# Block attention before a low-rank mixer: the masked fourth of the scores left out from step twelve on, with v and part of the mask turned

## The chip, the cores and the metric

The kernel runs on one core of one Trainium2 chip. The metric is the device time of one execution in microseconds (us). Four executions of the kernel before took 671.55, 673.17, 673.52 and 674.01 us; their median is 673.34 us.

The engines are named as in the profile: PE is TensorE (PEld its weight loads), DVE is VectorE, ACT is ScalarE, POOL is GpSimd and SP the queue that issues the DMA transfers. SBUF is the on-chip memory, PSUM the memory that PE writes its products to. Each has 128 partitions (rows).

## What is computed

Inputs are q, k and v of 4 batches, 8 heads, 768 positions and 64 features, a decay `lam` per head, and the weights of a mixer. The first half is linear attention with decay, written here in the reference's blocks:

```python
intra = einsum('bhic,bhjc->bhij', qb, kb) * Dmask      # Dmask[i,j] = lam**(i-j) for i >= j, else 0
intra = einsum('bhij,bhjd->bhid', intra, vb)
inter = einsum('bhid,bhde->bhie', qb * lam_pow, kv_state)
out[block] = intra + inter
kv_state = lam_block * kv_state + einsum('bhsd,bhse->bhde', kb * rev_pow, vb)
```

The output, as x of 4 x 768 x 512, goes through `u = x + (x^T U V)^T` (rank 32) and then `u + relu(u @ w_ch1) @ w_ch2` with an inner width of 2048.

What matters here is `Dmask`: a score whose key j comes after its query i is multiplied by zero.

## The kernel before

The kernel takes 128 positions at a time. With 4 batches of 6 such tiles there are 24 steps, numbered s = 0 to 23; c = s mod 6 is the place of the step in its batch. Two heads lie side by side in the 128 partitions of the transposed q and k: head 2a + x has pair number a = 0..3 and half x = 0, 1. The attention stage of all 24 steps ends at about 121 us; after it come two large matrix products of the mixer (lines 717 to 899), in which the kernel spends the rest of its time. The change doesn't touch those.

One step issues the following, in an order that `pieces` (lines 554 to 581) writes out by hand. Every engine works through its own instructions strictly in that order.

- `prep(s+1)`, lines 349 to 367: PE transposes q and k of the next tile into PSUM (pq, pk), ACT copies them to SBUF (qt, kt). The loads of later tiles are issued on SP.
- `scale`: POOL multiplies q and k by powers of the decay (qs, ks).
- `fade` (line 392): ACT multiplies the state by the decay of one tile, in four small instructions (faded).
- `mix` (line 514): PE forms the rank-32 part of a tile seven steps back (pu), DVE adds it to that tile (x_nat, line 517).
- `low`, `low_rows`: only where c = 0, the projection of the batch before (pp, L469), split by DVE and ACT into parts.
- `intra(s)` (line 453): PE multiplies the masked scores sm with v into px; ACT copies px to SBUF (x_nat, line 458).
- `state(s)` (line 418): for c < 5, PE forms k^T v (pkv), DVE adds it to the faded state (kv). The PSUM bank of pkv is that of pk, so pkv starts only after ACT has copied kt. Then the next tile of v is loaded into the buffer that has come free.
- `scores(s+1)` (line 400): PE multiplies k with q into pss, keys in the partitions and queries in the columns.
- `aside`: pieces of work for the weights of the large products (lines 149 to 224) on DVE; their ACT part follows as `late`.
- `inter(s+1)` (line 441): PE multiplies qs with the state kv into px.
- `masked(s+1)` (line 409): DVE multiplies pss with the mask, one instruction for each half x, and writes sm.
- `turn` (lines 531 to 547): PE transposes the finished tile (put), DVE splits it (ut, u_hl), ACT and POOL finish the split one step later (u_hl at line 550, u_d).

All these matmuls are in fp32, and each leaves two records of weight load and two of matmul in the trace (the transposes one). A matmul whose weights are 64 x 64 uses one quarter of the array; which one follows from the partitions of its operands and of its output. From step 12 on the scores of a tile are already formed by 16 such matmuls, two halves of keys for each head, each with all 128 queries; before step 12 by 8 matmuls with 128 keys each:

```python
for rows in half if s >= 2 * NT else [slice(0, P)]:
    nc.tensor.matmul(
        out=pss[rows, x, a, :], lhsT=kt[half[x], a, rows],
        rhs=qt[half[x], a, :], start=True, stop=True,
```

For keys 64 to 127 the first 64 of these 128 columns are scores that the mask sets to zero: a fourth of the tile's scores.

Of the kernel before, what the change touches and what calls it, by code (L numbers as in the profile page):

```python
# [8 lines left out]
FP32 = mybir.dt.float32  # L9
# [5 lines left out]
P = 128  # L15
# [3 lines left out]
def kernel(  # L19
# [28 lines left out]
    nc = tc.nc  # L48

    B, H, S, D = q.shape  # L50
    HP = H // 2
    NT = S // P
# [45 lines left out]
    def tmp(name):  # L98
        return wconv.tile([P, C], FP32, tag="tmp", bufs=3, name=name)
# [146 lines left out]
    att = att_ctx.enter_context(tc.tile_pool(name="att", bufs=1))  # L246
# [5 lines left out]
    def two_banks(name, tag):  # L252
        return psf.tile([P, 2, N], FP32, tag=tag, name=name)
# [12 lines left out]
    raw = {}  # L266
# [30 lines left out]
    mask = consts.tile([P, 2, HP, P], FP32, name="mask")  # L297
# [33 lines left out]

    xs = {}
    st = {}
    kv = {}
    half = [slice(0, D), slice(D, P)]
# [55 lines left out]

    def scores(s):
        qt, kt = st[s]["qt"], st[s]["kt"]
        st[s]["pss"] = pss = two_banks("pss", "pss").rearrange("p x (a i) -> p x a i", a=HP)
        for a in range(HP):
            for x in range(2):
                for rows in half if s >= 2 * NT else [slice(0, P)]:
                    nc.tensor.matmul(  # L400
                        out=pss[rows, x, a, :], lhsT=kt[half[x], a, rows],
                        rhs=qt[half[x], a, :], start=True, stop=True,
                    )

    def masked(s):
        pss = st[s].pop("pss")
        st[s]["sm"] = sm = att.tile([P, 2, HP, P], FP32, tag="sm", bufs=1, name="sm")
        for x in range(2):
            nc.vector.tensor_tensor(out=sm[:, x], in0=pss[:, x], in1=mask[:, x], op=ALU.mult)  # L409

    def state(s):
# [34 lines left out]
    def intra(s):  # L446
        first = s % NT == 0
        sm, vr, px = st[s]["sm"], raw[s, "v"], st[s]["px"]
        px = px[:, :, 0 : HP * D].rearrange("p x (a e) -> p x a e", a=HP)
        for a in range(HP):  # L450
            for x in range(2):
                for t in range(2):
                    nc.tensor.matmul(  # L453
                        out=px[half[t], x, a, :], lhsT=sm[:, x, a, half[t]],
                        rhs=vr[:, 2 * a + x, :], start=(first and a == 0), stop=(a == HP - 1),
                    )
        xs[s] = x_pool.tile([P, C], FP32, tag="x", name="x_nat")
        nc.scalar.copy(xs[s].rearrange("p (a x e) -> p x a e", a=HP, x=2), px)


    pps = {}
# [57 lines left out]
    uhl, ud, turned = {}, {}, {}  # L519
# [42 lines left out]
    for s in range(NS):  # L562
        b, c = divmod(s, NT)
        done = s - NT - 1
        more = s + 1 < NS
        step = [("prep", s + 1), ("scale", s + 1)] * more + [("fade", s)] * (c == 1)
        step += [("late", s - 1)] * (s == NT)
        step += [("mix", done)] * (0 <= done < NS - NT - 1)
        step += [("low", b - 1)] * (c == 0 and b > 0)
        step += [("low_rows", b - 1)] * (c == 0 and b > 0)  # L570
        step += [("intra", s)]
        step += [("next_of_low", b - 1)] * (c == 0 and b > 0)
        step += [("late", s)] * (s < NT - 1 or s == NT) + [("state", s)]
        step += [("next_of_low", b - 1)] * (c == 0 and b > 0)
        step += [("turned", done - 1)] * (done > 0) + [("late", s)] * (done >= 0)
        step += [("next_of_low", b - 1)] * (c == 0 and b > 0)
        step += [("scores", s + 1)] * more
        step += [("aside", s)] * (s >= 2 * NT)
        step += [("inter", s + 1), ("masked", s + 1)] * more
        step += [("fade", s + 1)] * (more and c > 0)  # L580
        step += [("aside", s)] * (s < 2 * NT)
        step += [("turn", done)] * (done >= 0 and done // TG < FG)
        pieces += step
    waiting = {name: list(range(NS)) for name in "qkv"}

    def load_next(name, engine=nc.sync):
# [3 lines left out]

    run = {
        "prep": prep, "fade": fade, "scores": scores, "masked": masked, "inter": inter,
        "intra": intra, "state": state,
        "low": low, "low_rows": low_rows, "next_of_low": next_of_low, "mix": mix, "turn": turn,
        "scale": scale, "turned": lambda s: turned.pop(s)(),
    }
    def v_steps():

# [186 lines left out]
    c0, b = NS - NT, B - 1  # L785
# [181 lines left out]
```

## Time and profile before

| what | value |
|---|---|
| median of four executions | 673.34 us |
| the profiled execution | 673.52 us, of which the span from first to last instruction is 671.7 us |
| granted PE clock | 1.000 |
| busy share of the span | PE 99%, DVE 74%, ACT 41%, POOL 17% |
| one step of the attention stage (71.84 to 76.58 us) | 4.74 us, of which DVE is busy 4.71 and ACT 4.09 |
| scores, steps 12 to 23 | 192 matmuls of 64x128 (384 records), one record 0.269 us |
| masking, steps 12 to 23 | 24 DVE instructions of 128x512, 0.680 us each |
| ACT copy of 128x512 from PSUM | 0.585 to 0.592 us |

How to read it: the length of a matmul record is its passage through the pipeline, and records overlap, so what a block of matmuls costs is the time from its first start to the first start of the next block. A busy engine need not be the bound: PE also counts as busy while matmuls trickle. The number in brackets behind an instruction is idle time of its engine before it, with the instruction that ended it.

### The profile page before, as it was taken

Reading aid. Unit: us, or ns where it says so; the run is one execution under the profiler, and the core shown is the slowest. Engines: PE = TensorE matmul, PEld = TensorE weight load, DVE = VectorE, ACT = ScalarE, POOL = GpSimd, SP = SyncE. Lnnn points to the kernel's source line nnn. Section 1 sums busy time; section 2 is a strip of 40 time slices with the busy share of each in tenths; the row PEclk is TensorE's granted clock in tenths of the full one; section 3 lists DMA queues with packets and bytes.
Section 4 is the critical chain, followed back from the end, with each engine's and each line's share of the span. In section 5 each row is a group of like instructions: output and inputs, shape, how many; then the busy total and the mean of one; then the engine's idle time right before and its main releaser. Section 6 shows DMA issues by size and latency. Waiting matters only on the chain.

```text
span 671.7 us, 13171 instructions
## 1 busy us (share of the span) xinstructions
PE 664.8 (99%) x5124; PEld 544.9 (81%) x5124; DVE 497.2 (74%) x873; ACT 277.7 (41%) x517; POOL 112.6 (17%) x92
## 2 busy tenths in 40 slices
PE   9999999999999999999999999999999999999997
PEld 8887989788888888888888888888888888888885
DVE  5688999877999777777797265786586775865854
ACT  4675767554555444444454121332222322322320
POOL 4555657340000000000000000030030300300300
PEclk9999999999999999999999999999999999999999
DMA  9999994254676555555587899854363363542421
GB/s 204 216 221 223 243 242 118 89 210 156 238 279 235 204 203 204 204 203 204 203 282 256 313 318 390 284 197 138 94 211 102 111 203 94 162 152 95 160 91 62
DMA packets 131775, 131.27 MB, mean 195 GB/s; under 512 B 81346, under 2 KB 89794, under 8 KB 131714
## 3 DMA queue, kind: packets, MB, share of 16 engines
q1 hardware_dynamic: 130656, 130.18, 61.2%
q8 instruction: 40, 0.66, 0.4%
q10 hardware_dynamic: 1058, 0.26, 0.2%
q14 instruction: 21, 0.17, 0.1%
HBM read 80.09 MB, written 50.33 MB: 194 GB/s over the span
## 4 chain that ended last, share of the span: by engine, by line
PE 96%; DVE 2%; ACT 1%; issue 0%; DVEq 0%; ACTq 0%
PE pz L731 27%; PE pz L866 13%; PE pz L864 13%; PE pd L741 13%; PE pd L868 13%; PE pss L400 3%; PE px L453 3%; PE put L531 2%; PE pq L355 1%; PE pkv L418 1%; PE px L441 1%; PE pk L355 1%; PE pp L469 1%; DVE sm L409 1%; PE pu L514 1%; PE idle L343 0%
## 5 line engine op out<-in xcount | busy, mean ns | idle before, releaser
L731 PE MATMUL pz<-u_hl,w 128*128 128x512 f32 x768 | 190.4, 398 | 0.0
L731 PEld LDWEIGHTS pz<-u_hl,w 128*128 128x128 f32 x768 | 144.1, 188 | 35.4 <-issue 0.4
L866 PE MATMUL pz<-w_hl,m 128*128 128x512 f32 x384 | 151.1, 396 | 0.0
L864 PE MATMUL pz<-w_hl,m 128*128 128x512 f32 x384 | 151.0, 397 | 0.0
L868 PE MATMUL pd<-w_d,m 128*128 128x512 f32 x384 | 149.5, 397 | 0.0
L847 ACT ACTIVATE m<-mt 128x512 fp32r<-128x512 f32 x96 | 60.6, 632 | 197.0 <-PE pd L868 137.7
L848 DVE SCALAR_TENSOR_TENSOR m<-rm,m 128x512 fp32r<-128x512 f32 x96 | 71.4, 745 | 50.0 <-ACT m L847 49.7
L893 POOL TENSOR_TENSOR o<-o,u 128x512 f32<-128x512 f32 x20 | 29.8, 1526 | 447.4 <-DVE o L889 447.4
L746 DVE SCALAR_TENSOR_TENSOR r<-pd,r 128x512 f32<-128x512 f32 x96 | 61.8, 685 | 53.3 <-ACT r L737 38.8
L741 PE MATMUL pd<-u_d,w 128*128 128x512 f32 x384 | 98.6, 397 | 0.0
L737 ACT ACTIVATE r<-pz 128x512 f32<-128x512 f32 x96 | 52.1, 595 | 93.0 <-PE pz L731 92.9
L866 PEld LDWEIGHTS pz<-w_hl,m 128*128 128x128 f32 x384 | 72.4, 188 | 17.6
L864 PEld LDWEIGHTS pz<-w_hl,m 128*128 128x128 f32 x384 | 72.3, 188 | 17.6
L868 PEld LDWEIGHTS pd<-w_d,m 128*128 128x128 f32 x384 | 72.3, 188 | 17.6
L741 PEld LDWEIGHTS pd<-u_d,w 128*128 128x128 f32 x384 | 72.1, 188 | 17.3
L849 DVE SCALAR_TENSOR_TENSOR m<-m 128x512 fp32r<-128x512 f32 x96 | 69.0, 720 | 0.9
L846 DVE TENSOR_SCALAR mt<-rm 128x512 uint32<-128x512 uint32 x96 | 46.1, 481 | 31.0 <-DMA rm<-r_d 30.4
L409 DVE TENSOR_TENSOR sm<-pss,mask 128x512 f32<-128x512 f32 x48 | 30.8, 684 | 7.0 <-PE pss L400 6.8
L212 ACT CAST w<-wt 128x512 fp32r<-128x512 f32 x32 | 19.8, 620 | 30.5 <-DVE wt L209 23.4
L453 PEld LDWEIGHTS px<-vraw,sm 128*64 128x64 f32 x768 | 24.6, 138 | 5.9 <-DVE sm L409 2.3
L383 POOL TENSOR_TENSOR qs<-qt,powq 128x512 f32<-128x512 f32 x20 | 25.9, 1296 | 20.2 <-ACT qt L358 18.6
L453 PE MATMUL px<-vraw,sm 128*64 128x64 f32 x768 | 28.2, 226 | 0.4 <-DVE sm L409 0.3
(88 smaller groups left out, 681.8 us busy)
## 6 DMA issues: line engine op xcount, KB each, us to landing
r_d<-r SPq DMA_DIRECT2D x96, 256.0 KB, 2.7
rm<-r_d SPq DMA_DIRECT2D x96, 256.0 KB, 2.7
words<-in_moe_w_ch_dram SPq DMA_DIRECT2D x30, 512.0 KB, 4.5
w_d<-w SPq DMA_DIRECT2D x16, 768.0 KB, 3.3
w_hl<-w_d SPq DMA_DIRECT2D x16, 512.0 KB, 6.2
vraw<-in_v_dram SPq DMA_DIRECT2D x24, 256.0 KB, 5.1
u_d<-x_nat SPq DMA_DIRECT2D x24, 256.0 KB, 3.7
u<-u_d SPq DMA_DIRECT2D x24, 256.0 KB, 4.2
```

What stands on the lines that cost most here:

```text
L453: nc.tensor.matmul(out=px[half[t], x, a, :], lhsT=sm[:, x, a, half[t]], rhs=vr[:, 2 * a + x, :], start=(first and a == 0), stop=(a == HP - 1),
L731: nc.tensor.matmul(out=acc[g][0], lhsT=w[:, n, ct, :], rhs=uhl[g][:, n, ct, :], start=(ct == 0 and n == 0), stop=(ct == CT - 1 and n == 1),)
L737: nc.scalar.mul(rs[g], acc[g][0], 4096.0 + 1.0)
L741: nc.tensor.matmul(out=acc[g][1], lhsT=w[:, 2, ct, :], rhs=ud[g][:, ct, :], start=(ct == 0), stop=(ct == CT - 1),)
L746: nc.vector.scalar_tensor_tensor(rs[g], acc[g][1], 4096.0, rs[g], ALU.mult, ALU.add)
L846: nc.vector.tensor_scalar(t.bitcast(U32), r.bitcast(U32), HI, None, ALU.bitwise_and)
L847: nc.scalar.activation(out=m[:, 0], in_=t, func=AF.Relu)
L848: nc.vector.scalar_tensor_tensor(m[:, 1], r, 0.0, hi, ALU.max, ALU.subtract)
L849: nc.vector.scalar_tensor_tensor(m[:, 2], hi, E, low, ALU.mult, ALU.subtract)
L864: nc.tensor.matmul(out=pz, lhsT=m[:, 0, cols], rhs=hl[:, 0], start=first, stop=False)
L866: nc.tensor.matmul(out=pz, lhsT=m[:, 1, cols], rhs=hl[:, 1], start=False, stop=end)
L868: nc.tensor.matmul(out=pd, lhsT=m[:, 2, cols], rhs=dd, start=first, stop=end)
```

## The change

From step 12 on (`TURNED`):

- `scores` leaves out the block of keys 64 to 127 by queries 0 to 63. The keys 0 to 63 still get 128 columns, the keys 64 to 127 get 64.
- For odd pairs of heads (a = 1, 3) the two halves of keys trade places in PSUM: keys 64 to 127 lie in partitions 0 to 63 and the others in 64 to 127. In the loop over output halves o, even pairs have the long matmul first and odd pairs the short one. Each quarter of the array gets two long and two short matmuls.
- The part of pss that is not written keeps what an earlier step left there; the mask multiplies it by zero. For that pss becomes one tile for all steps, `sums`.
- The mask's odd pairs are turned the same way, once: ACT copies their halves crosswise into a spare tile in steps 9 and 10, and back in step 11 (`turn_mask`).
- v of the odd pairs must be turned too, in every step from 12 on: `turn_v`, two ACT copies of 64 partitions by 256 elements. They are issued behind `intra` of the step before; for the second step of a batch (c = 1: steps 13 and 19) they are issued in the step itself, behind the copies of q and k and ahead of `fade`.
- `intra` takes the pairs in the order 0, 2, 1, 3 (in all steps) and reads the turned v for odd pairs.
- `masked` is one DVE instruction of 128x1024 instead of two of 128x512.

In the order of the built program this adds 27 ACT instructions (24 of turn_v, 3 of turn_mask) and takes 12 away on DVE; the counts of matmuls stay. The second half of `intra` now also waits for ACT, and SP's load of v into a used buffer waits for ACT besides PE.

```diff
+    sums = two_banks("pss", "pss")
+    TURNED = 2 * NT
...
-        st[s]["pss"] = pss = two_banks("pss", "pss").rearrange("p x (a i) -> p x a i", a=HP)
+        st[s]["pss"] = pss = sums.rearrange("p x (a i) -> p x a i", a=HP)
         for a in range(HP):
             for x in range(2):
-                for rows in half if s >= 2 * NT else [slice(0, P)]:
+                for o in range(2) if s >= TURNED else ():
+                    i = o if a % 2 == 0 else 1 - o
+                    cols = slice(i * D, P)
                     nc.tensor.matmul(
-                        out=pss[rows, x, a, :], lhsT=kt[half[x], a, rows],
+                        out=pss[half[o], x, a, cols], lhsT=kt[half[x], a, half[i]],
+                        rhs=qt[half[x], a, cols], start=True, stop=True,
+                    )
+                if s < TURNED:
+                    nc.tensor.matmul(
+                        out=pss[:, x, a, :], lhsT=kt[half[x], a, :],
                         rhs=qt[half[x], a, :], start=True, stop=True,
                     )
...
-        for x in range(2):
+        for x in [slice(0, 2)] if s >= TURNED else [slice(0, 1), slice(1, 2)]:
             nc.vector.tensor_tensor(out=sm[:, x], in0=pss[:, x], in1=mask[:, x], op=ALU.mult)
...
-        for a in range(HP):
+        for a in (0, 2, 1, 3):
...
-                        rhs=vr[:, 2 * a + x, :], start=(first and a == 0), stop=(a == HP - 1),
+                        rhs=vs[s][:, a // 2, x, :] if s >= TURNED and a % 2 else vr[:, 2 * a + x, :],
...
+    def turn_v(s):
+        odd = raw[s, "v"].rearrange("p (j b x) d -> p j b x d", b=2, x=2)[:, :, 1]
+        vs[s] = att.tile([P, HP // 2, 2, D], FP32, tag="vs", name="vs")
+        for i in range(2):
+            nc.scalar.copy(vs[s][half[1 - i]], odd[half[i]])
+
+    odd_mask = mask[:, :, 1::2, :]
+
+    def turn_mask(n):
+        if n == 0:
+            held.append(tmp("turned").rearrange("p (x j i) -> p x j i", x=2, j=HP // 2))
+        if n < 2:
+            nc.scalar.copy(held[0][half[1 - n]], odd_mask[half[n]])
+        else:
+            nc.scalar.copy(odd_mask, held.pop())
...
+        step += [("turn_v", s)] * (c == 1 and s >= TURNED) + [("fade", s)] * (c == 1)
...
+        step += [("turn_mask", 2)] * (s == TURNED - 1)
+        step += [("intra", s)] + [("turn_v", s + 1)] * (more and s + 1 >= TURNED and c > 0)
+        step += [("turn_mask", s - TURNED + 3)] * (TURNED - 3 <= s < TURNED - 1)
```

More of the change, by code (lines that the diff above doesn't have):

```diff
@@ L326 @@
     r_pool = None
+    sums = two_banks("pss", "pss")
+    TURNED = 2 * NT
     xs = {}
+    vs, held = {}, []
     st = {}
@@ L454, in intra @@
                         out=px[half[t], x, a, :], lhsT=sm[:, x, a, half[t]],
-                        rhs=vr[:, 2 * a + x, :], start=(first and a == 0), stop=(a == HP - 1),
+                        rhs=vs[s][:, a // 2, x, :] if s >= TURNED and a % 2 else vr[:, 2 * a + x, :],
+                        start=(first and a == 0), stop=(a == HP - 1),
                     )
@@ L458, in intra @@
         nc.scalar.copy(xs[s].rearrange("p (a x e) -> p x a e", a=HP, x=2), px)
+        vs.pop(s, None)
+    def turn_v(s):
[11 more added lines that the diff above has]
+            nc.scalar.copy(odd_mask, held.pop())
     pps = {}
@@ L565 @@
         more = s + 1 < NS
-        step = [("prep", s + 1), ("scale", s + 1)] * more + [("fade", s)] * (c == 1)
+        step = [("prep", s + 1), ("scale", s + 1)] * more
+        step += [("turn_v", s)] * (c == 1 and s >= TURNED) + [("fade", s)] * (c == 1)
         step += [("late", s - 1)] * (s == NT)
@@ L570 @@
         step += [("low_rows", b - 1)] * (c == 0 and b > 0)
-        step += [("intra", s)]
+        step += [("turn_mask", 2)] * (s == TURNED - 1)
+        step += [("intra", s)] + [("turn_v", s + 1)] * (more and s + 1 >= TURNED and c > 0)
+        step += [("turn_mask", s - TURNED + 3)] * (TURNED - 3 <= s < TURNED - 1)
         step += [("next_of_low", b - 1)] * (c == 0 and b > 0)
@@ L594 @@
         "low": low, "low_rows": low_rows, "next_of_low": next_of_low, "mix": mix, "turn": turn,
-        "scale": scale, "turned": lambda s: turned.pop(s)(),
+        "turn_v": turn_v, "turn_mask": turn_mask, "scale": scale, "turned": lambda s: turned.pop(s)(),
     }
```

## The prediction

> **What bounds the kernel now.** I read four views in this order: the page's engine totals, the busy time by stretches (one stretch per step of the attention stage), the timelines of TensorE (PE) and ScalarE (ACT) around steps 9 and 13, and the chain of waits.
>
> The totals and two stretches first. The columns of a stretch are its length, then busy time of PE, its weight loads, VectorE (DVE), ACT and POOL.
>
> ```profile
> PE 664.8 (99%) x5124; PEld 544.9 (81%) x5124; DVE 497.2 (74%) x873; ACT 277.7 (41%) x517; POOL 112.6 (17%) x92
> ...
> 71.84:76.58 4.74, 4.74 (x126) 4.36 (x126) 4.71 (x8) 4.09 (x14) 3.93 (x4) 1.00 1.08 263
> 81.31:86.15 4.84, 4.82 (x127) 4.37 (x126) 4.80 (x8) 3.25 (x10) 2.78 (x2) 1.00 1.01 247
> ```
>
> Only the attention stage, to about 121 us, is touched. There PE sets the pace of most steps, one every 4.74 us, but DVE is nearly as full (4.71 and 4.80), and ACT fills 4.09 of the first. A saving on PE therefore helps only where neither of the two is late next.
>
> PE, with start, length, line and tile:
>
> ```profile
> 71.84 1.15 PE L453 MATMUL px<-vraw,sm 128*64 128x64 f32 x32
> 72.83 0.64 PE L418 MATMUL pkv<-vraw,ks 128*64 128x64 f32 x16
> 73.39 1.10 PE L400 MATMUL pss<-qt,kt 64*64 64x128 f32 x32
> 74.32 0.64 PE L441 MATMUL px<-kv,qs 64*64 64x64 f32 x32
> 74.89 0.66 PE L531 MATMUL put<-ident,x_nat 128*128 128x128 f32 x4
> ```
>
> Scores occupy 0.93 us (73.39 to 74.32). The product with the state (L441) has the same 32 records on the same four 64x64 quarters of the array (corners, below), with 64 columns instead of 128, and takes 0.57.
>
> ACT at step 9 has no idle time between 52.78 and the end of kt, and PE waits for that kt:
>
> ```profile
> 52.78 0.58 ACT L458 COPY x_nat<-px 128x512 f32<-128x512 f32 x1 [2.19 <-PE pss L400]
> 53.27 0.63 ACT L550 ACTIVATE u_hl<-ut 128x512 fp32r<-128x512 f32 x1
> ...
> 55.17 1.05 ACT L392 ACTIVATE faded<-kv,powq 128x64 f32<-128x64 f32 x4
> 56.13 0.56 ACT L358 COPY qt<-pq 128x512 f32<-128x512 f32 x1
> 56.60 0.57 ACT L358 COPY kt<-pk 128x512 f32<-128x512 f32 x1
> ...
> 57.22 0.69 PE L418 MATMUL pkv<-vraw,ks 128*64 128x64 f32 x16 [0.28 <-ACT kt L358]
> ```
>
> ACT at step 13, with two prices of small copies:
>
> ```profile
> 71.34 0.59 ACT L358 COPY qt<-pq 128x512 f32<-128x512 f32 x1
> 71.82 0.59 ACT L358 COPY kt<-pk 128x512 f32<-128x512 f32 x1
> ...
> L621 ACT CAST vp<-vt 32x384 fp32r<-32x384 f32 x2 | 1.0, 510 | 0.0
> L358 ACT COPY qt<-pq 128x256 f32<-128x256 f32 x2 | 0.7, 372 | 1.7 <-PE pq L355 1.6
> ```
>
> The chain of waits from 78 to 87 us runs through DVE, not PE:
>
> ```profile
> 78.74 1.21 DVE w L217
> 79.95 1.20 DVE sm L409 x2
> ...
> 84.07 1.42 DVE sc L160
> 85.49 1.21 DVE sm L409 x2
> 86.74 1.03 PE px L453 x28
> ```
>
> **Scores.** Blocks 12 to 23 keep 16 matmuls each, but half of them have 64 columns; each corner gets two long and two short ones. The 32 records come in eight rounds of four. Starts take 1.10 - 0.27 (one record) = 0.83 over seven gaps at 128 columns, 0.64 - 0.22 = 0.42 over seven at 64: 0.119 and 0.060, the first inflated by the fill of the first round. I take 0.05 per shortened round, four of them: 0.20 us a block, if each corner runs through its own list. The other bound is that records start in program order over the corners. With 0.11 a long and 0.06 a short record, the first corner of a pair of heads starts at 0, 0.11, 0.22 (short), 0.28 (short), and its neighbour's short ones stand behind its long ones: 0.01, 0.12, then long at 0.23 and 0.34; the second pair likewise from 0.35, but with its short ones at 0.45 and 0.51 behind the neighbour's last long one, to 0.80 in all. Now it is 8 x 0.11 = 0.88, with own lists 0.68. So 0.08 saved. Bounds: 0 and 0.23.
>
> That all 32 records fit 0.93 us speaks for own lists: 16 matmuls leave 32 records, so two for each corner in turn; if the second of a corner held up the next corner's first, sixteen times 0.11 would already be 1.76 us. The Trainium skill ("TensorE: Matmul & The Clock Gate", Part 3, what overlaps and what doesn't) says the opposite: matmuls start and end in strict program order. By that rule the sum below would be about +1.7 us instead of +0.7; the row does not fit it unless the two records are interleaved over the corners, which the trace doesn't show.
>
> Of the twelve blocks:
> - Block 12 (62.32) gives 0: the transposes behind it (63.84) wait for DVE's x_nat (63.10 to 63.78), queued behind a 1.60 us conversion.
> - Block 13 (68.66) gives 0.1: its masked scores end at 71.79, PE takes them at 71.84.
> - Block 16 (82.86) gives 0.05: DVE runs without a break from 78.32 to 88.6, so only the shorter masking counts.
> - Block 23 (117.28) costs 0.1: DVE starts masking at 118.45 behind a conversion and PE now needs all of it, not the first half.
> - The other eight give 0.20 each, 1.6. Sum: -1.65.
>
> **Masking.** One 128x1024 instruction instead of two of 128x512. Two take 1.28, starting 0.61 apart; one saves the second's fixed part, about 0.06 (bounds 0 and 0.13). But the first product no longer starts on the first half. Both are inside the figures above.
>
> **Turned mask.** Three ACT copies: 64x512 at steps 9 and 10, 128x512 at 11. ACT rows with 512 elements from SBUF take 0.61 to 0.62 and, on part of the partitions, don't overlap with the next (68.79, 69.41, 70.04). The first stands between x_nat (52.78) and u_hl: qt, kt and so pkv slip by 0.62 and everything behind them, DVE's masking included. Price +0.6 (bounds 0.5, with overlap, and 0.62). The second is before an idle of 2.56 us, the third before one of 0.63 (x_nat at 62.44): nothing. If that cover went, 0.6 more each.
>
> **Turned v.** Two ACT copies of 64x256 a step. By elements: 0.256 at 128, 0.372 at 256, 0.510 at 384, 0.614 at 512; I take 0.41 each, 0.82 the pair, as the row L621 (other partitions, two behind one another, 1.03 for x2) is nearest. Bounds 0.28 (overlapping) and 0.61.
> - In the second step of batches three and four (13 and 19) they are queued behind qt and kt, and the products of odd heads wait for them. kt starts at 71.82, the next op 0.5 later: 72.32 + 0.82 + 0.05 = 73.19. PE would want them half-way through the product: 71.84 + 0.49 = 72.33. Stall 0.86; at step 19 likewise (101.50 and 101.52). Behind the stalled matmuls stand pkv and the next scores; ACT's faded and x_nat slip with them, DVE's state update too. Sum +1.7. Bounds 0.55 each at 0.28 a copy, 1.25 at 0.61.
> - In the other ten steps they follow x_nat. ACT idles 0.62 before qt at 76.08, 0.45 at 80.81, and kt ends 0.41 before pkv. That covers 0.82 and the 0.20 by which PE asks sooner, except at step 14, where a 0.51 us weight copy (78.79) shares the slack: +0.1. Without that cover each step would pay what exceeds about 1.0.
> - The load of v into a freed buffer now also waits for these copies, on SP, with loads of q and k behind it. The copies end before the products that read them, and SP waited for those already: nothing.
>
> **Head order 0, 2, 1, 3** moves no instruction past another tile's: 0 by itself; it is what gives the odd heads 0.49 us more time.
>
> **Sum.** -1.65 + 0.6 + 1.7 + 0.1 = +0.75, say +0.7 us. The profiled execution took 673.52 (span 671.7 and 1.8 around it), so 674.2; it lies 0.18 above the median of the runs, and against that median (which I use from here on) it is 674.0: no difference to speak of, as 0.3% is 2.0 us, about what a measurement of this kernel can tell from no change. After 121 us PE is the bound throughout, so the shift is passed on.
>
> **Rivals.**
> 1. *Corners wait for each other.* Scores give 0.08 a block instead of 0.20: eight times 0.12 and 0.05 at block 13 are lost, +1.7, 675.0. Against it, the 32 records in 0.93 us. Still within 0.3%.
> 2. *Slower: ACT's copies on half the partitions cost what 512 elements cost,* 0.61. Place: steps 13 and 19, 1.25 each instead of 0.86 (+0.8), and in the six other steps that have a state product behind kt (14 to 16, 20 to 22) a pair of 1.22 instead of 0.82 overruns the slack by some 0.2 (+1.1): +2.6, 675.9. It decides from about 0.56 a copy on. For it: ACT is the engine that PE already waits for at step 9. Against it: the price falls with the elements in every row shown.
> 3. *Faster: the turned copies are hidden.* No stall at 13 and 19, overlap elsewhere, the mask's copy caught up: between -1.65 and -2.4 (twelve blocks at 0.20), 670.9 to 671.7. Against it: ACT's order puts them behind qt and kt.
> 4. *The change doesn't do what it says:* a short matmul takes a long one's round, blocks stay at 0.93 and 1.7 of the gain are gone: +2.4, 675.7. Against it, L441's 0.57.
>
> **How the numbers follow.** Forecast 45%, rival 1 20%, rival 2 14%, rival 3 13%, rival 4 8%. Faster by over 0.3% needs rival 3 and the better end of it, or gains that no row shows: 0.13. Slower needs rival 2 or 4: 0.22. The forecast and rival 1 stay within: 0.65. The range takes the forecast's bounds and rivals 1 and 4 and leaves out the far part of 2 and 3: 672.1 to 675.9.
>
> **What would show it.** Right: scores from start to the next product 0.72 instead of 0.93; a wait of PE for ACT's turned v of 0.8 us in exactly two steps; pkv at step 10 0.6 later; the first product of the large stage 0.7 later than at 120.8. Wrong: turned copies far from 0.41, no PE wait at 13 and 19, ACT late at kt in many steps, or a DVE that is late at more masks than that of 85.49.

## The result, and the profile after

The changed kernel takes 674.09 us (median of 42 runs; 68 runs of the kernel before beside it: 672.65). The ratio is 1.0016 with a 95% interval of 1.0010 to 1.0023, so it is 0.7 to 1.5 us slower, around 1.1. Predicted were +0.7 us and 674.0.

The profiled execution of the changed kernel took 672.93 us (span 671.1), that of the kernel before 673.52 (671.7). The two profiles have the opposite sign of the timed ratio: single executions of either kernel spread over 4 us, which is more than the change. So the traces are compared step by step here, and the sum is taken from the timed ratio. A step is the time from the first start of `intra` to that of the next.

Totals, from the page of the kernel after:

```profile
PE 663.8 (99%) x5124; PEld 543.7 (81%) x5124; DVE 495.1 (74%) x861; ACT 289.5 (43%) x544; POOL 111.0 (17%) x92
```

ACT has its 27 instructions more and 12 us more work, DVE 12 instructions less.

PE at step 13 in the timeline of the kernel after (start, length, line and tile, idle time before it):

```profile
70.77 0.69 PE L463 MATMUL px<-vraw,sm 128*64 128x64 f32 x16
72.27 0.69 PE L463 MATMUL px<-vs,sm 128*64 128x64 f32 x16 [0.81 <-ACT vs L476]
72.78 0.64 PE L428 MATMUL pkv<-vraw,ks 128*64 128x64 f32 x16
73.35 0.90 PE L405 MATMUL pss<-qt,kt 64*64 64x128 f32 x32
74.11 0.69 PE L451 MATMUL px<-kv,qs 64*64 64x64 f32 x32
```

ACT just before, with the two turned copies behind kt:

```profile
70.79 0.59 ACT L361 COPY kt<-pk 128x512 f32<-128x512 f32 x1
71.39 0.82 ACT L476 COPY vs<-vraw 64x256 f32<-64x256 f32 x2
72.24 1.06 ACT L395 ACTIVATE faded<-kv,powq 128x64 f32<-128x64 f32 x4
```

The second half of `intra` starts 1.50 us after the first instead of 0.52 (76.42 to 76.93 in the next step): a stall of 0.98, and 0.99 at step 19. The list of waits of the kernel after, from 71 us to the end of the stage (who waits for whom, us in total, times, longest), names it twice:

```profile
PEld px L463 <- ACT vs L476: 1.9, 2, 1.0
PE px L463 <- ACT vs L476: 1.6, 2, 0.8
```

The scores now take 0.76 us up to the product behind them (73.35 to 74.11) instead of 0.92. But that product is 0.05 slower, 0.62 to the next block instead of 0.57. An undisturbed step went from 4.74 to 4.62. The stretches of steps 13 to 16, with columns as in the prediction:

```profile
70.77:76.42 5.65, 4.84 (x127) 4.33 (x126) 4.71 (x7) 5.54 (x17) 3.61 (x4) 1.00 0.85 211
76.42:81.04 4.62, 4.62 (x126) 4.25 (x125) 4.39 (x7) 4.12 (x11) 3.81 (x4) 1.00 1.06 259
81.04:85.86 4.82, 4.82 (x126) 4.33 (x125) 4.65 (x8) 4.57 (x13) 2.59 (x3) 1.00 0.87 213
85.86:90.48 4.62, 4.62 (x126) 4.25 (x125) 4.34 (x8) 3.90 (x9) 3.55 (x4) 1.00 1.01 242
```

Steps 13 to 22 in us, and the rest up to the first product of the large stage (pz), from the first starts in both traces:

| step | 13 | 14 | 15 | 16 | 17 | 18 | 19 | 20 | 21 | 22 | 23 to pz | sum |
|---|---|---|---|---|---|---|---|---|---|---|---|---|
| before | 4.74 | 4.73 | 4.83 | 5.26 | 5.39 | 4.74 | 4.73 | 4.74 | 4.74 | 3.86 | 1.16 | 48.92 |
| after | 5.65 | 4.62 | 4.82 | 4.62 | 5.25 | 4.68 | 5.65 | 4.63 | 4.62 | 3.95 | 1.08 | 49.57 |

So +0.65 us arise from step 13 on. From pz to the end it is 551.0 and 550.8. If the other 0.4 or so is real (the interval leaves 0 to 0.9), it lies in steps 9 to 12, where the other copies of the change stand. Step 9 alone took between 4.95 and 8.48 us in the profiles of this study (the kernel with exchanged loads, below, apart), with short ones and long ones both among kernels that have the mask copy and among those that don't, so no pair of profiles can show a difference of 0.4 there.

### The profile page after: what moved, and what is told of

Read it like the earlier page. It is cut to its first block, busy times and chain, and to the rows that moved or that the text cites. A ratio compares the mean times of both kernels' runs of the same rounds, so it can differ in the third digit from the quotient of the medians.

```text
span 671.1 us, 13191 instructions
## 1 busy us (share of the span) xinstructions
PE 663.8 (99%) x5124; PEld 543.7 (81%) x5124; DVE 495.1 (74%) x861; ACT 289.5 (43%) x544; POOL 111.0 (17%) x92
## 4 chain that ended last, share of the span: by engine, by line
PE 96%; ACT 2%; DVE 1%; DMA 1%; issue 0%; DVEq 0%; ACTq 0%
PE pz L762 27%; PE pz L897 13%; PE pz L895 13%; PE pd L772 13%; PE pd L899 13%; PE px L463 4%; PE pss L410 2%; PE pq L358 2%; PE px L451 1%; PE put L559 1%; PE pk L358 1%; PE pkv L428 1%; PE pp L497 1%; PE pss L405 1%; PE pu L542 1%; DMA qraw<-in_q_dram 1%
## 5 line engine op out<-in xcount | busy, mean ns | idle before, releaser
L419 DVE TENSOR_TENSOR sm<-pss,mask 128x512 f32<-128x512 f32 (+1 forms) x36 | 30.1, 863 | 7.3 <-PE pss L410 6.4
L186 DVE SCALAR_TENSOR_TENSOR sc<-words,sc 128x512 uint32<-128x512 uint32 (+2 forms) x34 | 23.4, 687 | 1.1 <-ACT sc L168 1.1
L579 POOL TENSOR_TENSOR u_d<-u_hl 128x512 fp32r<-128x512 f32 x16 | 21.0, 1312 | 18.9 <-ACT u_hl L578 12.4
```

## The experiments

All are set against the kernel before, timed on the same chip; against the changed kernel they stand by the difference of the two ratios (0.001 is 0.67 us), which is uncertain by some 0.9 us. "Stage" is the time from `intra` of step 13 to pz: 49.57 in the changed kernel.

**Scores: full width, and long ones on two corners only.**

```diff
-                    cols = slice(i * D, P)
+                    cols = slice(0, P)
```

> The changed kernel, but every score matmul of steps 12 to 23 has 128 columns again (cols = slice(0, P)); turned v, turned mask, single masking and head order stay. My theory (the shortening is worth something, but less than I predicted: in the changed kernel's trace 0.76 us from the first start of a block to the next product's instead of 0.92, of which the next product gives 0.05 back): the block takes 0.92 to 0.93 again, an undisturbed step 4.73 instead of 4.62, and the kernel is 0.9 to 1.5 us slower than the changed one, 2.0 to 2.6 slower than the one before (ratio 1.003 to 1.004). By the 0.20 a block of the prediction it would be 1.7 slower than the changed one, 2.8 slower than before. Rival, that a short matmul takes a long one's round: same as the changed kernel, ratio 1.0016.

Measured: ratio 1.0036 (1.0025 to 1.0048), 1.3 us slower than the changed kernel. The stage takes 50.47, 0.90 more. The block takes 0.92 again, undisturbed steps 4.73 to 4.74. So the shortening is real (rival 4 of the prediction falls), but is worth a good 0.1 in a step, not 0.20. Outside the stage, step 12 takes 5.90 instead of 4.81, here and in the next kernel. There DVE's line 191 starts 0.12 us behind an instruction of POOL (64.18 and 64.06) and takes 1.72 us; in the changed kernel it starts 0.09 ahead of that instruction (63.98 and 64.07) and takes 0.68. That is a collision of the kind which the last part of this section describes, and in these profiles the shorter block 12 avoids it. The kernel before, of full width too, doesn't meet it in its profile (0.68, step 12 4.74).

```diff
-                    i = o if a % 2 == 0 else 1 - o
+                    i = o
```

> The changed kernel with i = o for all pairs of heads: the long score matmuls of all four pairs go to the two corners that write partitions 0 to 63, the short ones to the other two. The number of matmuls and columns is the same; what is written for odd pairs is another arrangement than mask and v expect. My theory, that each corner of the array runs through its own list: two corners have eight long records as before, so the block takes 0.92 to 0.93 as in the kernel before, and the kernel is like the one with full columns, 0.9 to 1.5 us slower than the changed one. Rival, that records start in program order over the corners, with a long one holding up its neighbours: 0.88 by the prediction's steps for eight long ones in a row, also no gain, but then the short ones lie evenly between the long ones, 0.11 apart, and don't run ahead. Rival, that only the sum of columns counts: 0.76 as in the changed kernel, same time.

Measured: ratio 1.0034 (1.0023 to 1.0046), stage 50.44: like full width, as the theory of own lists has it, although a fourth of the columns is left out. Its PE timeline shows the lists themselves:

```profile
74.65 0.99 PE L405 MATMUL pss<-qt,kt 64*64 64x128 f32 x30
75.41 0.28 PE L451 MATMUL px<-kv,qs 64*64 64x64 f32 x2
75.46 0.28 PE L405 MATMUL pss<-qt,kt 64*64 64x128 f32 x2
75.52 0.69 PE L451 MATMUL px<-kv,qs 64*64 64x64 f32 x30
```

The two corners with short records only begin the next product at 75.41, while the last two long ones of the scores start at 75.46. The order of the program holds within a corner, not over the corners; for PE, "strictly in that order" in the description of the kernel before is true of one corner only. Without turned halves the shortening would gain nothing; that is what the turning is for.

**Turned v left out, and the old order of heads.**

```diff
-                        rhs=vs[s][:, a // 2, x, :] if s >= TURNED and a % 2 else vr[:, 2 * a + x, :],
+                        rhs=vr[:, 2 * a + x, :],
...
-        step += [("turn_v", s)] * (c == 1 and s >= TURNED) + [("fade", s)] * (c == 1)
+        step += [("fade", s)] * (c == 1)
...
-        step += [("intra", s)] + [("turn_v", s + 1)] * (more and s + 1 >= TURNED and c > 0)
+        step += [("intra", s)]
```

> The changed kernel without the copies that turn v: odd heads read v as it was loaded. This leaves out the turning of v (24 ACT copies), so the products of odd heads take v's rows in another order. My theory (the copies cost two stalls of PE, 0.9 us each, at steps 13 and 19, and nothing in the other ten steps): steps 13 to 14 and 19 to 20 take 4.62 instead of 5.4 to 5.65, the other steps stay at 4.62, and the kernel is 1.7 to 1.9 us faster than the changed one, 0.6 to 0.8 faster than before (ratio 0.999). Rival, that the ACT time of the copies also delays kt in the other steps: more than 2.2 faster than the changed one, and the other steps shorter than 4.62. Rival, that DVE is late next where the stall goes: less than 1.0 faster than the changed one.

Measured: ratio 0.9984 (0.9974 to 0.9995), 2.1 us faster than the changed kernel. Steps 13 and 19 take 4.66 and 4.64 instead of 5.65. The others of the stage stay within 0.04, with two exceptions. Step 17 takes 5.18 instead of 5.25: there the copies push ACT's u_hl and with it qt, which PE waits for. And step 15 takes 5.38 instead of 4.82, so the stage, 48.13, gains only 1.44. The cause of that is a DVE instruction that met POOL, as it does in the kernel before (shown further down). So the copies cost two stalls and 0.07 in step 17, and the other steps of the stage hide them.

```diff
-        for a in (0, 2, 1, 3):
+        for a in range(HP):
```

> The changed kernel with the pairs of heads in intra in the order 0, 1, 2, 3 again, one look. My theory: the first turned pair is then wanted a quarter into the product instead of half-way, 0.25 us sooner, so the two stalls at steps 13 and 19 grow from 0.9 to 1.15 us each, steps 13 to 14 and 19 to 20 take 5.9 instead of 5.65, and the other steps stay as they are. Rival, that the order alone moves other steps: differences there.

Measured in a single execution: steps 13 and 19 take 5.88 each instead of 5.65, 0.23 more; all others from 14 on are as in the changed kernel. The new order is worth what it puts between the need and the copy, and nothing else.

**Turned mask left out.**

```diff
-        step += [("turn_mask", 2)] * (s == TURNED - 1)
...
-        step += [("turn_mask", s - TURNED + 3)] * (TURNED - 3 <= s < TURNED - 1)
```

> The changed kernel without the three copies that turn the mask's odd pairs in steps 9 to 11: the odd pairs of steps 12 to 23 are multiplied with the unturned mask. My theory: the first copy pushes qt and kt of step 9 by 0.6 and PE with them, so this kernel is 0.5 to 0.6 faster than the changed one, 0.5 slower than before (ratio 1.0008), and PE's start of pkv at step 10 comes 0.5 to 0.6 sooner after x_nat of step 9. Rival, that the delay is caught up behind it, since DVE sets the pace between steps 9 and 13: same as the changed one within 0.2, with the difference gone by the masking of step 12.

Measured: ratio 0.9995 (0.9983 to 1.0008), 1.4 us faster than the changed kernel. In the profiles step 10 takes 4.95 instead of 5.47, 0.52 less, as expected. In the changed kernel the copy and a wait for kt stand there; without the copy PE doesn't wait:

```profile
52.10 0.62 ACT L484 COPY turned<-mask 64x512 f32<-64x512 f32 x1
...
56.70 0.69 PE L428 MATMUL pkv<-vraw,ks 128*64 128x64 f32 x16 [0.30 <-ACT kt L361]
```

(Only profiles whose step 9 took 4.95 can be compared so. The kernel before, without the copy, has 5.46 in step 10 too, behind its disturbed step 9.) But step 11 takes 5.62 instead of 5.25, and step 12 4.69 instead of 4.81, so by the start of step 13 only 0.27 is left. The price at its place is shown; what reaches the end (0.3 by these profiles, 1.4 +- 0.9 by the times) is open.

**Short ones first.** Why is a block worth 0.115 and not 0.20? My first theory was the order within the block.

```diff
-        for a in range(HP):
+        for n in range(HP):
...
+                    a = ((1, 3, 0, 2), (0, 2, 1, 3))[o][n]
```

> The changed kernel with another order inside the block of scores: each corner of the array gets its two short matmuls first and its two long ones last (pairs 1, 3, 0, 2 for the one output half, 0, 2, 1, 3 for the other). My theory: in the changed kernel two of the four corners end on short records, and the product with the state behind the block can call its first weights only after a wait that stands in front of it, so the last shortening is lost (start to next start 0.76 instead of the predicted 0.72, and the next product 0.48 instead of 0.43 from its first to its last start). With a long record last in every corner the block takes 0.72 and the next product 0.43 again: an undisturbed step 4.53 instead of 4.62, and the kernel 0.7 to 0.9 us faster than the changed one, 0.2 to 0.4 slower than the one before (ratio 1.0005). Rival, that the first records of a block are spaced by weight loads whatever their columns are, so that short ones in front save nothing: block 0.76 or more, same time as the changed kernel.

Measured: ratio 1.0028 (1.0019 to 1.0037). Undisturbed steps are 4.62, block 0.76, stage 49.58: nothing won (by the times it is 0.8 slower than the changed kernel, within the uncertainty), and my theory falls. But the last record of the block now starts 0.63 after its first, and the next product still starts at 0.76. What it waits for is in the DVE timeline of the changed kernel:

```profile
71.95 0.68 DVE L545 TENSOR_TENSOR x_nat<-pu,x_nat 128x512 f32<-128x512 f32 x1
73.53 0.42 DVE L436 TENSOR_TENSOR kv<-pkv,faded 128x256 f32<-128x256 f32 x1 [0.91 <-PE pkv L428]
73.87 1.03 DVE L209 TENSOR_SCALAR wt<-wf 128x512 uint32<-128x512 uint32 x1
```

The state kv can't start before pkv's last record has ended (73.42) and runs to 73.96; PE's wait ends at 74.05, the first weights are called at 74.07, the product starts at 74.11. In the kernel before, the same wait ended at 74.13, 0.08 before PE called the weights at 74.21. In steps 14, 20 and 21 the picture is the same: counted from the block's first start, the wait ends at 0.70 in both kernels, and the weights are called at 0.82 before and at 0.73 after. So the room was 0.08 to 0.12 us, and the shorter block has used it up. The next experiments test this.

**Transposes of the finished tile ahead of the product with the state,** in the changed kernel and in the one before:

```diff
+        step += [("put_first", done)] * (s >= TURNED and done // TG < FG)
         step += [("inter", s + 1), ("masked", s + 1)] * more
```

(`put_first` issues the four transposes; `turn` keeps its other work at its old place.)

> The changed kernel with one move on PE: from step 12 on the four transposes of the finished tile (put) stand ahead of the product with the state (inter) instead of behind it; the other engines keep their order. My theory, new from the trace of the changed kernel: the shortened scores end before DVE has written the state kv (pkv's last record ends at 73.42, DVE's kv runs from 73.53 to 73.96, PE's wait ends at 74.05, the first matmul of inter at 74.11), so kv sets the start of inter and a further shortening is worth nothing. With 0.5 us of transposes in between, kv is early: an undisturbed step takes 4.53 to 4.55 instead of 4.62, and the kernel is 0.6 to 0.9 us faster than the changed one, 0.2 to 0.5 slower than the one before (ratio 1.0005). Rival, that the loss lies in how weights of 64x64 matmuls are called one after another and not in kv: steps stay at 4.62. Rival, that DVE, busy 4.4 us in such a step, is late next: steps at 4.6.

> The kernel before with the move of the transposes alone (from step 12 on ahead of the product with the state). My theory: with scores of full width kv is done 0.08 us before PE wants it (PE's wait for it ends at 74.13, the first weights are called at 74.21), so there is nothing to win: undisturbed steps stay at 4.74 (4.72 to 4.75), the same time as before (ratio 1.000). It also shows once more the steps 9 to 12, where the profile of before had an idle stretch of ACT behind a transfer. Rival, that the order is better by itself, whatever the scores cost: steps 4.65 or less, 0.8 us faster or more.

Measured: ratios 1.0028 (1.0017 to 1.0039) and 1.0035 (1.0018 to 1.0051). Both expectations of the time failed: the move itself costs. Undisturbed steps take 4.84 instead of 4.62 in the changed kernel, and 5.05 instead of 4.74 in the kernel before, where nothing at all was to change. PE in the latter:

```profile
85.25 1.10 PE L400 MATMUL pss<-qt,kt 64*64 64x128 f32 x32
86.28 0.66 PE L528 MATMUL put<-ident,x_nat 128*128 128x128 f32 x4
86.87 0.69 PE L441 MATMUL px<-kv,qs 64*64 64x64 f32 x32
87.50 0.66 PE L355 MATMUL pq<-ident,qraw 128*128 128x128 f32 x4
```

The move makes two changes more between matmuls on quarters of the array and matmuls on all of it. PE's rows name no other engine there, and the four gaps from scores to pk grow by 0.05 to 0.11 each, so I take +0.31 as the price of both; what PE does in that time the trace doesn't show. The Trainium skill ("TensorEngine Tiling (Array Packing)", Key Properties) says that changing the tiling mode drains the engine; these steps agree with that, at about 0.15 us a change.

Yet the pair answers the question. With transposes behind the scores, kv is no longer what follows them. Then the full-width block takes 1.03 to the next start (85.25 to 86.28) and the shortened one 0.83 (85.50 to 86.33), and the steps differ by 0.21: the 0.20 of the prediction, in full.

**The product with the state reads an older state.**

```diff
-                        rhs=kv[s][half[x], a, :], start=(a == 0), stop=False,
+                        rhs=kv[s - (s >= TURNED and s % NT > 1)][half[x], a, :], start=(a == 0), stop=False,
```

> The changed kernel, but from step 12 on the product with the state (inter) reads the state of one step earlier wherever the batch has one (places 2 to 5 of a batch). The work and its order are the same on every engine; what is left out is the dependence on the newest state, so the output is that of an older one. My theory (DVE's kv sets when inter starts, 74.11 in the trace of the changed kernel, although the scores give way earlier): blocks of scores behind which such a product follows take 0.72 to 0.73 instead of 0.76 and the product 0.43 instead of 0.48 from first to last start, an undisturbed step 4.53 to 4.55 instead of 4.62, and the kernel is 0.4 to 0.7 us faster than the changed one (eight steps have such a product), 0.4 to 0.7 slower than the one before (ratio 1.0008). Rival, that the weights of the product are called late for another reason, such as POOL's qs or the short records that end the block: steps stay at 4.62, time as the changed one.

Measured in its PE timeline:

```profile
82.57 0.90 PE L405 MATMUL pss<-qt,kt 64*64 64x128 f32 x32
83.29 0.65 PE L451 MATMUL px<-kv,qs 64*64 64x64 f32 x32
83.87 0.66 PE L559 MATMUL put<-ident,x_nat 128*128 128x128 f32 x4
```

The block takes 0.72 and the product 0.58; undisturbed steps take 4.53 to 4.56, the stage 49.11. Nothing was changed but the dependence on kv, so kv is what held the product in the changed kernel, and what made it slower to fill (0.62 to the next block there). The timed ratio, 1.0007 (0.9991 to 1.0023), lies where it was expected, but its interval is too wide to add anything. Its profile also holds the widest disturbance but one at step 9 (8.44 us), in which ACT waited for a write of u_d that landed late:

```profile
55.90 0.58 ACT L469 COPY x_nat<-px 128x512 f32<-128x512 f32 x1 [3.31 <-DMA u_d<-x_nat]
```

**v turned a step earlier for steps 13 and 19.**

```diff
-        step += [("turn_v", s)] * (c == 1 and s >= TURNED) + [("fade", s)] * (c == 1)
+        step += [("turn_v", s + 1)] * (c == 0 and s >= TURNED) + [("fade", s)] * (c == 1)
...
-        vs[s] = att.tile([P, HP // 2, 2, D], FP32, tag="vs", name="vs")
+        vs[s] = att.tile([P, HP // 2, 2, D], FP32, tag="vs", bufs=2, name="vs")
```

> The changed kernel with the copies that turn v of steps 13 and 19 moved one step ahead on ACT, behind the copies of q and k in steps 12 and 18, into an idle time of ACT of 2.2 us in the changed kernel's trace (64.95 to 67.16); the tile vs has two buffers for it. My theory (the stall at 13 and 19 is only the place in ACT's order): both stalls vanish, steps 13 to 14 and 19 to 20 take 4.62 to 4.65 instead of 5.65, and the kernel is 1.8 to 2.0 us faster than the changed one, 0.7 to 0.9 faster than the one before (ratio 0.999), as the kernel without turned v was. Rival, that the copies push ACT's casts of the batch's end and with them the copies of q and k: less than 1.0 faster than the changed one, with waits for ACT elsewhere in these steps.

Measured: ratio 0.9989 (0.9979 to 0.9999), 0.7 us faster than the kernel before and 1.8 than the changed one. Steps 13 and 19 take 4.64 and 4.63. Step 12 pays for a part (5.53 instead of 4.81), because the load of v had not landed and ACT waited for it:

```profile
66.29 0.82 ACT L476 COPY vs<-vraw 64x256 f32<-64x256 f32 x2 [1.88 <-DMA vraw<-in_v_dram]
```

So the stall was the place in ACT's order, not the work. This version is faster than both kernels, than the kernel before by 0.1 to 1.4 us.

With the transposes moved as well:

> Two edits of the runs before together: the changed kernel with v of steps 13 and 19 turned a step earlier, and with the transposes of the finished tile ahead of the product with the state from step 12 on. My theory: the two gains are at different places of PE's path and add up, 1.8 and 0.6 to 0.9 us: 2.4 to 2.7 us faster than the changed one, 1.2 to 1.6 faster than the one before (ratio 0.9977 to 0.9982). Rival, that with both out of the way DVE sets the pace of most steps: no more than the 0.75 us that the earlier turning of v alone won against the kernel before.

Measured: ratio 1.0018 (1.0004 to 1.0032), so the expectation failed. Undisturbed steps are 4.84 to 4.86, and step 19 (4.85) has no stall, so the changes of tiling take back more than the earlier turning gives. Steps 13 and 14 (6.67 and 5.39) are disturbed in this profile: ACT waits 2.40 us for a late write of u_d. It can't show what the earlier turning does there.

**No copies: odd pairs loaded with exchanged halves.**

```diff
+            for j in range(0, n, 4):
+                engine.dma_start(
+                    out=t[:, h + j : h + j + 2, :],
+                    in_=rows[j : j + 2].rearrange("h p d -> p h d"),
+                )
+            for i in range(2):
+                for j in range(2, n, 4):
+                    engine.dma_start(
+                        out=t[half[1 - i], h + j : h + j + 2, :],
+                        in_=rows[j : j + 2, half[i]].rearrange("h p d -> p h d"),
+                    )
```

> The masked fourth left out with no copies at all: k and v of the odd pairs of heads are loaded with their halves of 64 positions exchanged, in all steps (three DMAs for each load of k and v instead of one), and the mask's odd pairs are built in that arrangement at the start; turned v, turned mask and vs are gone, and the scores have two short matmuls first and two long ones last in each corner. Output the same. My theory (what the change lost are the two stalls and the copy at step 9; what it won is 0.12 to 0.2 a block): no ACT copies more than before, scores as with the short ones first, 1.5 to 2.5 us faster than the kernel before (ratio 0.9963 to 0.9978). Rival, that the additional DMAs (64 more on SP, half as large) make loads of q, k or v late in some steps: same as before or slower, with waits of PE for kraw, qraw or vraw, at the start above all.

Measured: 782.35 us, ratio 1.164 (1.162 to 1.166); steps 13 to 20 take 7.4 to 11.1 us. As written it issues six transfers for a load, not three (the odd pairs are no neighbours, so each loop runs twice). The reason is in SP's timeline:

```profile
106.77 0.38 SPq L281 DMA_DIRECT2D qraw<-in_q_dram  x1
107.26 1.16 SPq L284 DMA_DIRECT2D kraw<-in_k_dram  x2
108.47 2.56 SPq L290 DMA_DIRECT2D kraw<-in_k_dram  x4
```

A transfer of 32 KB holds SP for 0.64 us, more than q's 256 KB in one piece (0.38). The twelve transfers of k and v in a step (eight of 32 KB and four of 64 KB) are over 7 us of SP's time, against a step of 4.6. The rival held. Its waits are there (PE waits 20 us in all for v), but they are not the largest of the attention stage: ACT waits 73 us in all for writes of u_d, which SP issues in the same queue.

**A collision that several of these kernels share.** The DVE instruction of line 160 and POOL's u_d at 84 us, in the timeline of the kernel before:

```profile
83.71 1.50 POOL L551 TENSOR_TENSOR u_d<-u_hl 128x512 fp32r<-128x512 f32 x1 [0.96 <-ACT u_hl L550]
...
83.99 1.50 DVE L160 TENSOR_SCALAR sc<-words 128x512 uint32<-128x512 uint32 x1
```

Then in that of the changed kernel:

```profile
83.69 0.63 ACT L578 ACTIVATE u_hl<-ut 128x512 fp32r<-128x512 f32 x1
83.92 0.42 DVE L160 TENSOR_SCALAR sc<-words 128x512 uint32<-128x512 uint32 x1
...
84.40 1.28 POOL L579 TENSOR_TENSOR u_d<-u_hl 128x512 fp32r<-128x512 f32 x1 [1.41 <-DVE sc L160]
```

DVE's instruction takes 0.42 alone and 1.50 beside a u_d that has already begun. In the changed kernel the turned copies stand ahead of u_hl on ACT (83.69 instead of 83.00), so u_d can start only at 84.40 and DVE is first. (The bracket names DVE because its instruction ended last, at 84.34; u_hl, which u_d reads, ended at 84.32.) The kernel with exchanged loads apart, it is 1.50 in all three kernels that have no turned copies (before, the transposes moved in before, turned v left out), and 0.42 in the ten that have them. It delays the masking for step 16. The kernel before starts `intra` of that step on the first masked half and then waits for the second, so the loss stands in its step 16 (5.26 instead of 4.74); with one masking it stands in step 15, as where turned v was left out (5.38 instead of 4.82). The Trainium skill ("SBUF — State Buffer", SBUF: two separate sides) states a rule for this: DVE and POOL share a pair of ports, and of two instructions that need it (DVE needs it in some of its modes) the one that starts first keeps it to its end. The rows agree in the order: u_d begins first and ends at 85.21, and the DVE instruction ends 0.28 later. That is less than the 0.42 it takes alone, so by these rows not all of it was held up.

## Why the prediction was right

The time was right (+0.7 forecast, +1.1 measured, "within 0.3%"), but that is in part luck: the gain of the scores was mis-sized by 0.8 us, and 0.5 of that came back from a collision that the prediction didn't name. From step 13 on the terms of the prediction sum to +0.27: two stalls +1.72, eight blocks -1.60, blocks 16 and 23 +0.05, step 14 +0.1. Measured are +0.65:

| term | predicted | measured |
|---|---|---|
| stalls at steps 13 and 19 | +1.72 | +1.97 |
| eight blocks of scores | -1.60 | -0.79 |
| blocks 16 and 23 | +0.05 | +0.08 |
| copy of v at step 14 | +0.1 | 0 |
| DVE's line 160 at step 16 | not named | -0.53 |
| step 23 to pz | 0 | -0.08 |

(Step 16 is divided by giving its block the 0.11 of steps 14 and 20.)

- *Turned v, steps 13 and 19: right.* 0.41 a copy was forecast and measured (0.82 the pair), the two don't overlap, and exactly two steps wait. The stall was mis-sized by 0.12 each, mostly because the copies start 0.60 behind kt's start (70.79 to 71.39) and not 0.5; from kt to faded the ACT timeline of the kernel before had 0.62 (71.82 to 72.44).
- *The ten other steps hidden: right* but for 0.07 in step 17 instead of 0.1 in step 14, shown by leaving the copies out.
- *Scores, "0.20 us a block, if each corner runs through its own list": the mechanism was right, the size wrong.* The corners do run through own lists (the uneven kernel), and the block itself can be 0.72 (the older state) or 0.20 shorter (the transposes moved). The rule of the Trainium skill that the prediction weighed ("TensorE: Matmul & The Clock Gate", Part 3, what overlaps and what doesn't: start and end in program order) does not hold here between corners, with 75.41 ahead of 75.46. What failed is the step from the block to the path. I put -0.20 on PE's path without asking what the next product waits for besides PE. Its state comes from pkv, which stands in front of the same block, through 0.42 us of DVE, and that had 0.08 to 0.12 us to spare. This holds for six of the eight blocks (14, 15, 17, 20, 21, 22). The other two had other limits: block 18 is followed by transposes and is 0.20 shorter, but step 17 keeps only 0.14 of it, as ACT's copies push qt there; and block 19's product starts after 0.72, but step 18 wins only 0.06, as DVE masks that block behind vp, until 100.36, and `intra` starts at 100.42. Rival 1 had nearly the measured number (0.08 a block) for a cause that was not there.
- *Block 13 at 0.1: not seen.* Its step 12 takes 4.81 instead of 4.74.
- *DVE's share: block 16 at 0.05 and block 23 at +0.1: right* (step 15 -0.01, step 22 +0.09). The long run of DVE that limited the block of step 16 was rightly seen, but I took the 1.42 us of line 160 in it as its cost. It was a collision with POOL, and the copies on ACT, which I counted as cost only, ended it.
- *Turned mask, +0.6: 0.52 at its place.* How much of it reaches the end is open. The prediction didn't see that the same copies shorten step 11, where another instruction of DVE meets POOL: line 186 takes 1.27 to 1.60 us and step 11 5.53 to 5.87 in the three kernels without them (before, the transposes moved in before, turned mask left out), 0.68 and 5.18 to 5.39 in the ten that have them (1.02 in one of these, the older state). Whether "block 12 gives 0" holds can't be told apart from this.
- *Head order: right,* 0.23 a stall.
- *"The first product of the large stage 0.7 later than at 120.8": not seen* (120.34). The profile of before had lost 0.8 in step 9, where ACT stood still until 52.78; the kernel of before with the transposes moved, which has the same instructions up to there, lost 3.5. I took a disturbance of one execution for the kernel's own pace.

## What to carry to other kernels

When a block on the busiest engine gets shorter, look for the result that was made in front of the block and is wanted behind it: its way through another engine is a floor that the engine totals don't show, and its spare time (here 0.08 to 0.12 us) is about all that the shortening can give. Work put on an engine with idle time costs only where something is queued behind it and wanted at once; moving two of twelve pairs of copies to a place where ACT idles turned this change from a loss of some 1.1 us into a gain of some 0.7. Order and neighbours price an instruction: read its row once alone and once beside the engine it collides with before calling a duration its cost.

## What the runs showed of the hardware

- Matmuls on different quarters of the array overtake each other, across blocks of different lines too, by 0.05 us in the uneven kernel.
- Two changes more between 64x64 and full-array matmuls cost 0.31 us a step in the kernel before; in the changed one, +0.22 with the wait for kv gone at the same time.
- A DVE instruction of 0.42 us (line 160) takes 1.50 beside a POOL instruction that began 0.28 us sooner. One of 0.68 (line 191) takes 1.72 where POOL began 0.12 sooner, and keeps its 0.68 where it began 0.09 ahead of POOL.
- An ACT copy of 64x256 takes 0.41 us, no less than the copy of 128x256 in the prediction (0.37, but from PSUM); the two copies of the mask, SBUF to SBUF both, take 0.62 at 64x512 and 0.63 at 128x512. Half the partitions save nothing.
- SP is held 0.64 us by the issue of a 32 KB transfer of k, and 0.38 us by the one of 256 KB of q beside it.
- One late write to DRAM at step 9 moves a whole execution by up to 3.5 us, and with it the sign of a comparison of two profiles.
